# Two attention blocks on one core: K transposed partly in full 128-row tiles, one semaphore and one wait for K and V

## The chip, the core and the metric

The kernel runs on one core of a Trainium2 chip. A core has five engines with instruction streams of their own: TensorE (matmuls, "PE"), VectorE ("DVE"), ScalarE ("ACT"), GpSimd ("POOL") and SyncE ("SP", which here only issues DMAs). They meet through semaphores. Sixteen DMA engines move data between the device's memory (HBM) and the on-chip buffers: SBUF, from which the engines read, and PSUM (8 banks), into which TensorE writes. The metric is the time of one execution on the device in microseconds. Three timed executions of the kernel before took 883.15, 885.32 and 893.99 us; the median, 885.32 us, is its time.

## The reference

Two blocks A and B of the same shapes compute cross attention over a cache; their outputs stand side by side.

```python
B, Sq, D = 16, 64, 640
H, Sk, Dh = 32, 512, 128
def _A_ref(x, k_cache, v_cache, wq, wo):          # B likewise
    q = (x @ wq).reshape(B, Sq, H, Dh).transpose(0, 2, 1, 3)
    scores = jnp.einsum("bhqd,bhkd->bhqk", q, k_cache) * (Dh ** -0.5)
    p = _softmax(scores, axis=-1)
    o = jnp.einsum("bhqk,bhkd->bhqd", p, v_cache)
    return o.transpose(0, 2, 1, 3).reshape(B, Sq, H * Dh) @ wo
return jnp.concatenate([a, b], axis=-1)
```

All is bf16. K and V of the two blocks are 4 x 67.1 MB, most of the 289.41 MB that the kernel reads.

## The kernel before, in words

**Tiling.** A *step* is one head of two batch elements (j = 0 and 1), which share the 128 rows of a tile as two halves of 64 queries. A *macro step* m is two heads (sub = 0 and 1) of the same two batch elements; there are 256. Two macro steps make a *period*, of which there are 128. Eight macro steps (16 heads) make a group, eight groups (all 16 batch elements) a pass, and two passes (the two halves of the heads) a block.

**The operations** of a macro step, by the names that the plan gives them:
- LDK, LDV (SP, L679 and L681): load K and V of the macro step, 512 KB each, in two DMAs (one per j) of 256 KB into rings of 9 and 10 slots. Every half has a semaphore of its own, so the reader waits for two.
- KX (PE, L467): K comes with the keys on the partitions, two heads as rows 0 to 63 and 64 to 127. Each 64x128 piece is transposed by a matmul against the identity; the two heads use the two row halves of the array at the same time. 32 transposes a macro step, head 0 into PSUM bank 6, head 1 into bank 7.
- KE (DVE, L474): copies both banks into the ring `ktp_ring` (2 slots). There is one pair of banks, so the next KX waits for KE.
- SM(m, sub) (PE, L525): the scores of one head, two matmuls of 512 columns, one per j, side by side in the two column halves of the array; one PSUM bank of four for each head.
- MX (DVE, L534), EX (ACT, L540), RC2 (DVE, L546), NM (POOL, L554): maximum, exponential with its sum, reciprocal, and the product with it.
- TR2 (PE, L563): transposes the probabilities in eight full 128x128 tiles. TE2 (DVE, L570, odd macro steps) or TA2 (ACT, L575, even ones) copies them out.
- PV2 (PE, L585): probabilities times V, 16 matmuls of 64 columns; OE4 (ACT, L592) copies a period's result out.
- OP2 (PE, L600): the first 512 columns of the output projection, two matmuls. OX (PE, L610) makes the last 128 columns once a group, 16 matmuls. OVP, OXP (ACT) and OVF, OXF (DVE, L628, L633) copy or add them, and ST (ACT queue, L639) stores them.
- QJ (PE, L482) and QEJ make the queries of the first pass in its first 16 periods; QN (L497) and QEN make those of each next pass, in periods 0 to 111.

**The order** on each engine is written out by hand as tables in `Cfg`: `PE_T`, `ACT_T`, `DVE_T`, `POOL_T`, one row per operation of a period, with its macro step as an offset from the period's first, its sub, and a time in a period of 6.3 us. Only the order within a table sets an engine's program; the times are also used to say which operation reads or writes a buffer first. On PE a period is: SM(0,0), SM(0,1), SM(1,0), QJ, SM(1,1), KX of macro step +2, QN, OP2 -4, TR2 -2, OP2 -3, TR2 -1, KX +3, PV2 -2, OX -3, PV2 -1.

**Loads** are put in order by `build_plan` from due times (`LEAD`, 9 macro steps ahead, or when the ring's slot is free) and paced: every load gets a reckoned time (`DMA_US`), and waits until PE has come to the operation of that time.

**Waits.** `prune_waits` (L331 to L379) drops the waits that another one implies. `run_program` (L689) hangs the last of an operation's waits on its first instruction and issues the others as semaphore instructions ahead of it:

```python
if waits and not op.dma:
    attach = waits.pop()
for s, v in waits:
    e.wait_ge(sems[s], v * (16 if s[0].startswith("d_") else 1))
first, last = emitters[op.kind](e, op)
```

Of the kernel before, what the change touches and what calls it, by code (L numbers as in the profile page):

```python
# [15 lines left out]
class Cfg:  # L16
# [10 lines left out]
    STEP_US = (3.7, 3.2)  # L27
    DMA_US = dict(LDK=0.69, LDV=0.73, LDWQ=1.8, LDWO=1.8, LDX=1.3)
    START_US = -16.0
# [8 lines left out]
    PERIOD = 6.3  # L38
    PE_T = (("SM", 0, 0, 0.0), ("SM", 0, 1, 0.21), ("SM", 1, 0, 0.43), ("QJ", 2, 0, 0.57), ("SM", 1, 1, 0.64),
             ("KX", 2, 0, 2.11), ("QN", -2, 0, 2.12), ("OP2", -4, 0, 2.62), ("TR2", -2, 0, 2.9), ("OP2", -3, 0, 3.06),  # L40
             ("TR2", -1, 0, 3.73), ("KX", 3, 0, 4.07), ("PV2", -2, 0, 4.78), ("OX", -3, 0, 5.02),
             ("PV2", -1, 0, 6.12))
    ACT_T = (("OE4", -4, 0, 0.27), ("ST", -5, 0, 0.58), ("EX", 0, 0, 0.77), ("QEJ", 2, 0, 1.92), ("EX", 0, 1, 2.07),
             ("QEN", -2, 0, 2.33), ("TA2", -2, 0, 4.55), ("EX", 1, 0, 4.56), ("OVP", -3, 0, 5.53), ("EX", 1, 1, 5.92),
             ("OXP", -3, 0, 5.98))
    DVE_T = (("RC2", -1, 0, 0.19), ("MX", 0, 0, 0.5), ("MX", 0, 1, 0.92), ("MX", 1, 0, 1.02), ("KE", 2, 0, 2.2),
             ("MX", 1, 1, 2.54), ("RC2", 0, 0, 3.44), ("TE2", -1, 0, 4.69), ("KE", 3, 0, 5.24), ("OVF", -3, 0, 6.13),
             ("OXF", -3, 0, 6.19))
    POOL_T = (("NM", -1, 0, 0.42), ("NM", -1, 1, 1.5), ("NM", 0, 1, 5.63), ("NM", 0, 0, 5.65))
    ACT_TE = (0,)  # L50
    TRB = (0, 1)
    OXB = 2


class Op:
    __slots__ = ("eng", "kind", "idx", "reads", "writes", "sem", "count", "deps", "waits", "dur", "ts", "aux",
                 "dma")

    def __init__(self, eng, kind, idx, reads=(), writes=(), dur=0.0, ts=None, aux=None):
        self.eng = eng  # L60
        self.kind = kind
        self.idx = idx
        self.reads = tuple(reads)
        self.writes = tuple(writes)
        self.sem = None
        self.count = None
        self.deps = []
        self.waits = []
        self.dur = dur
        self.ts = ts  # L70
        self.aux = aux
        self.dma = kind in ("LDK", "LDV", "LDX", "LDWQ", "LDWO", "ST")


def build_plan(dims, cfg):
# [61 lines left out]
    def make_op(kind, m, sub, ts):  # L137
# [4 lines left out]
        if kind == "KX":  # L142
            return mk("pe", "KX", m, [("kn", m % cfg.NKB, 0), ("kn", m % cfg.NKB, 1), ("ident",)], [("KTB",)], ts)
        if kind == "KE":
# [36 lines left out]
        if kind == "PV2":  # L181
            return mk("pe", "PV2", m, [("pT", m % cfg.NT), ("v", m % cfg.NVB, 0), ("v", m % cfg.NVB, 1)], [("QOB",)],
                      ts)
        if kind == "OE4":
# [69 lines left out]
    for m in range(NMAC):  # L254
        for kind, ring, n_ring, cons, tb in (("LDK", "kn", cfg.NKB, "KX", 1), ("LDV", "v", cfg.NVB, "PV2", 2)):
            ready = at[cons, m - n_ring, 0] if m >= n_ring else NEG
            for j in range(2):
                add(ready, at[cons, m, 0], cfg.LEAD, tb + 0.1 * j, kind, (m, j), [(ring, m % n_ring, j)], (m, j))

# [17 lines left out]
    def sem_key(op):  # L277
        if op.kind in ("LDK", "LDV"):
            return ("d_" + op.kind[2:].lower(), op.writes[0][1], op.aux[1])
        if op.kind == "LDX":  # L280
            return ("d_x", op.aux[1])
        if op.kind in ("LDWQ", "LDWO"):
            return ("d_" + op.kind[2:].lower(), op.writes[0][1])
        if op.kind == "ST":
            return ("d_out",)
        if op.kind in ("INIT1", "INIT2"):
            return ("s_init",)
        return ("s_" + op.kind.lower(),)
# [7 lines left out]
    for eng in ENGINES:  # L296
        for op in progs[eng]:
            if not op.dma:
                assign(op)
    for op in sorted((o for e in ENGINES for o in progs[e] if o.dma), key=lambda o: (o.ts, o.aux)):  # L300
        assign(op)
# [29 lines left out]
def prune_waits(progs):  # L331
# [7 lines left out]
    while done < total:  # L339
        progress = False  # L340
        for eng in ENGINES:
            prog = progs[eng]
            while pc[eng] < len(prog):
# [10 lines left out]
                for w in list(cand):  # L354
                    for o in keep:
                        if o != w and snap[o].get(w[0], 0) >= w[1]:
                            keep.remove(w)
                            break
                op.waits = keep
                for w in keep:  # L360
# [21 lines left out]
def mha_kernel(nc, blocks, out, cfg=None):  # L382
# [32 lines left out]
    with contextlib.ExitStack() as es:  # L415
        block = es.enter_context(nc.Block())

        def sb(name, shape, dt):
            return es.enter_context(nc.sbuf_tensor(name, shape, dt))
# [4 lines left out]
        xT_sb = sb("xT_sb", [128, KT, NBP * 128], BF16)  # L424
        kn_ring = sb("kn_ring", [128, NKB, 2, 8, DH], BF16)
        v_ring = sb("v_ring", [128, NVB, 2, 2, 4, DH], BF16)
        ktp_ring = sb("ktp_ring", [128, NKT, 2, 2, SK], BF16)
        qj_ring = sb("qj_ring", [128, NQ, G, 128], BF16)
# [19 lines left out]
        qo_ps = ps[:, QO_BANK, :]  # L448
        kt_ps = [ps[:, KT_BANK0 + hs, :].bitcast(BF16).rearrange("p (j s) -> p j s", j=2) for hs in range(2)]
        kt_all = ps[:, KT_BANK0:KT_BANK0 + 2, :].rearrange("p b s -> p (b s)").bitcast(BF16)  # L450

# [5 lines left out]

        ox_ps = s_bank(cfg.OXB)[:, 0:N1]

        def em_KX(e, op):  # L460
            m = op.idx
            first = last = None
            for j in range(2):
                for t8 in range(8):
                    for hs in range(2):
                        r = slice(64 * hs, 64 * hs + 64)
                        ins = e.transpose(kt_ps[hs][:, j, 64 * t8:64 * t8 + 64], kn_ring[r, m % NKB, j, t8, :],  # L467
                                          ident[r, 64 * hs:64 * hs + 64])
                        first = first or ins
                        last = ins  # L470
            return first, last

        def em_KE(e, op):
            ins = e.tensor_copy(ktp_ring[:, op.idx % NKT].rearrange("p hs j s -> p (hs j s)"), kt_all)  # L474
            return ins, ins
# [39 lines left out]
        def em_SM(e, op):  # L515
            m, sub = op.idx
            g = 2 * m + sub
            k = g // G
            if k < PPQ:
                q = qj_ring[:, k % NQ, g % G, :]  # L520
            else:
                q = qc_ring[:, qcell[k // PPQ, g % SPB, k % PPQ // (SPB // G)], :]
            first = last = None
            for j in range(2):
                ins = e.matmul(s_bank(g)[64 * j:64 * j + 64, :], q[:, 64 * j:64 * j + 64],  # L525
                               ktp_ring[:, m % NKT, sub, j, :], start=True, stop=True, tile_position=(0, 64 * j))
                first = first or ins
                last = ins
            return first, last
# [48 lines left out]
        def em_PV2(e, op):  # L578
            m = op.idx
            first = last = None  # L580
            for sub in range(2):
                for j in range(2):
                    for t in range(4):
                        col = (2 * (m % 2) + sub) * 128 + 64 * j
                        ins = e.matmul(qo_ps[:, col:col + 64], v_ring[:, m % NVB, j, sub, t, :],  # L585
                                       pT_ring[:, m % NT, sub, t, 64 * j:64 * j + 64], start=(t == 0), stop=(t == 3))
                        first = first or ins
                        last = ins
            return first, last
# [83 lines left out]
        def em_LDKV(e, op):  # L673
            m, j = op.aux
            blk, bp, grp, ps_, hh0 = step_info(2 * m)
            h0 = (ps_ % NHALF) * HH + hh0
            src = blocks[blk][2 if op.kind == "LDV" else 1][2 * bp + j, h0:h0 + 2]
            if op.kind == "LDV":
                ins = e.dma_start(v_ring[:, m % NVB, j], src.rearrange("g (p t) d -> p g t d", p=128))  # L679
            else:  # L680
                ins = e.dma_start(kn_ring[:, m % NKB, j], src.rearrange("hs (p t) d -> (hs p) t d", t=8))  # L681
            return ins, ins
# [3 lines left out]
                        OVP=em_OVP, OXP=em_OXP, OVF=em_OVF, OXF=em_OXF, ST=em_ST, INIT1=em_INIT1, INIT2=em_INIT2,  # L686
                        LDWQ=em_LDWQ, LDWO=em_LDWO, LDX=em_LDX, LDK=em_LDKV, LDV=em_LDKV)

        def run_program(e, prog, final_waits=()):  # L689
            for op in prog:  # L690
# [4 lines left out]
                for s, v in waits:  # L695
                    e.wait_ge(sems[s], v * (16 if s[0].startswith("d_") else 1))
                first, last = emitters[op.kind](e, op)
                if attach is not None:
                    s, v = attach
                    first.wait_op(sems[s], v * (16 if s[0].startswith("d_") else 1), "sem-ge")  # L700
                last.then_inc(sems[op.sem], 16 if op.dma else 1)
# [73 lines left out]
```

## Time and profile before

| what | value | where from |
|---|---|---|
| median of the timed executions | 885.32 us | the three times |
| profiled execution | 887.1 us, span 885.3 us | its own time; the span is from its first to its last instruction |
| mean granted TensorE clock | 0.996 | of full speed |
| PE, DVE, ACT, POOL busy | 94%, 82%, 74%, 47% of the span | the page, part 1 |
| KX, one matmul; one weight load | 191 ns; 95 ns, 8192 of each | groups at L467 |
| KE | 1215 ns, 256 of them | group at L474 |
| a 256 KB load of K or V | 5.7 us from issue to landing | DMA issues |
| HBM read | 289.41 MB; 336 GB/s moved in the mean | DMA parts |

A matmul's mean is its time from start to modelled end; matmuls overlap, so the rate is read from the distance between starts. "Busy" of a group is the union of its instructions' times. "Idle before" is the time its engine stood before them, with what ended it; "issue" there means that nothing in the profile explains it. The chain goes back from the last instruction to what released each one.

### The profile page before, as it was taken

The page shows a single profiled execution, that of the slowest core. Times are in us where ns is not written, and L with a number is a line of the kernel's source. Part 1 is how long each engine was busy: PE and PEld are TensorE (multiplying, and loading weights), DVE is VectorE, ACT ScalarE, POOL GpSimd, SP SyncE. Part 2 cuts the span into 40 slices and gives each one's busy share as a digit, 9 for nine tenths or more (in the row PEclk, how much of TensorE's full clock was granted, in tenths as well). Part 3 has the DMA queues.
Part 4 walks back from the last instruction along what each step waited for, and adds up shares of the span by engine and source line. Part 5 has one row for each costly group of instructions (what it writes and reads, how often), then busy time and mean ns, then how long its engine had stood idle before and what let it go on. Part 6 is the DMA issues. An engine that isn't in the chain of part 4 may idle for free.

```text
span 885.3 us, 40110 instructions
## 1 busy us (share of the span) xinstructions
PE 835.7 (94%) x17264; PEld 575.4 (65%) x17264; DVE 729.9 (82%) x1184; ACT 657.4 (74%) x1497; POOL 418.6 (47%) x518
## 2 busy tenths in 40 slices
PE   4989998999989999999999999999999999999897
PEld 3666775666656666665666666676666666766665
DVE  3667777888878888888888888888889889889996
ACT  2667777877877777777776787787788867877775
POOL 1333434544544454454444455455454544555454
PEclk8999999999999999999999999999999999999999
DMA  9999999999999999999999999999999999999980
GB/s 256 336 318 305 345 361 357 347 363 361 367 358 341 368 346 284 360 362 365 344 305 348 358 364 355 365 357 363 350 352 341 366 367 335 328 334 370 351 262 17
DMA packets 244847, 297.28 MB, mean 336 GB/s; under 512 B 27584, under 2 KB 179136, under 8 KB 244672
## 3 DMA queue, kind: packets, MB, share of 16 engines
q1 hardware_dynamic: 242368, 292.10, 98.9%
q8 instruction: 138, 2.26, 1.0%
q10 hardware_dynamic: 2304, 2.62, 0.8%
q14 instruction: 37, 0.30, 0.1%
HBM read 289.41 MB, written 2.62 MB: 330 GB/s over the span
## 4 chain that ended last, share of the span: by engine, by line
PE 87%; DMA 4%; DVE 4%; issue 3%; SPq 1%; ACT 0%; ACTq 0%
PE ps L467 16%; PE ps L585 14%; PE ps L497 14%; PE ps L525 14%; PE ps L563 12%; PE ps L600 12%; PE ps L610 3%; PE ps L482 2%; DVE ktp_ring L474 2%; DVE negmax L534 2%; DMA wq_sb<-in_A_wq_dram 1%; DMA kn_ring<-in_A_k_cache_dram 1%; DMA v_ring<-in_A_v_cache_dram 1%; SPq L679 0%; DVE pT_ring L570 0%
## 5 line engine op out<-in xcount | busy, mean ns | idle before, releaser
L554 POOL TENSOR_SCALAR pn_ring<-p_ring,recip 128x512 bf16<-128x512 bf16 x512 | 418.0, 846 | 458.7 <-DVE recip L546 358.2
L540 ACT ACTIVATE p_ring<-ps,negmax 128x512 bf16<-128x512 f32 x512 | 347.3, 684 | 75.6 <-DVE negmax L534 67.3
L534 DVE TENSOR_REDUCE negmax<-ps 128x1 f32<-128x512 f32 x512 | 328.2, 683 | 32.0 <-PE ps L525 27.4
L474 DVE COPY ktp_ring<-ps 128x2048 bf16<-128x2048 bf16 x256 | 311.1, 1215 | 32.6 <-PE ps L467 32.2
L467 PEld LDWEIGHTS ps<-ident,kn_ring 64*128 64x128 bf16 x8192 | 135.5, 95 | 80.5 <-issue 64.8
L467 PE MATMUL ps<-ident,kn_ring 64*128 64x64 bf16 x8192 | 167.5, 191 | 15.6 <-issue 9.2
L563 PEld LDWEIGHTS ps<-ident,pn_ring 128*128 128x128 bf16 x2048 | 135.3, 98 | 63.9 <-ACT p_ring L540 3.7
L585 PE MATMUL ps<-pT_ring,v_ring 128*128 128x64 bf16 x4096 | 151.7, 193 | 9.7 <-issue 8.2
L575 ACT ACTIVATE pT_ring<-ps 128x1024 bf16<-128x1024 bf16 x128 | 131.1, 1024 | 39.3 <-PE ps L563 38.8
L563 PE MATMUL ps<-ident,pn_ring 128*128 128x128 bf16 x2048 | 156.5, 219 | 2.5 <-issue 2.2
L570 DVE COPY pT_ring<-ps 128x1024 bf16<-128x1024 bf16 x128 | 88.3, 690 | 81.9 <-PE ps L563 81.9
L600 PE MATMUL ps<-wo_sb,oT_ring 128*128 128x512 bf16 x512 | 152.5, 379 | 3.2 <-issue 1.8
L497 PE MATMUL ps<-xT_sb,wq_sb 128*128 128x512 bf16 x560 | 141.0, 381 | 4.1 <-issue 4.1
L585 PEld LDWEIGHTS ps<-pT_ring,v_ring 128*128 128x128 bf16 x4096 | 131.6, 98 | 19.5 <-issue 11.1
L525 PE MATMUL ps<-ktp_ring,qc_ring 128*64 128x512 bf16 x896 | 122.5, 387 | 2.6 <-issue 2.4
L592 ACT ACTIVATE oT_ring<-ps 128x512 bf16<-128x512 f32 x128 | 76.4, 597 | 48.9 <-PE ps L585 40.0
L540 ACT ACTIVATION_READ_ACCUMULATOR p_ring<-ps,negmax 128x1 f32 x512 | 103.1, 201 | 0.0
L510 ACT ACTIVATE qc_ring<-ps 128x256 bf16<-128x256 f32 (+1 forms) x168 | 70.3, 453 | 43.7 <-PE ps L497 43.7
L497 PEld LDWEIGHTS ps<-xT_sb,wq_sb 128*128 128x128 bf16 x560 | 45.5, 98 | 50.5 <-issue 5.8
L600 PEld LDWEIGHTS ps<-wo_sb,oT_ring 128*128 128x128 bf16 x512 | 43.2, 98 | 31.6 <-issue 2.8
L525 PEld LDWEIGHTS ps<-ktp_ring,qc_ring 128*64 128x64 bf16 x896 | 37.3, 108 | 40.3 <-issue 25.8
L546 DVE RECIPROCAL recip<-rowsum 128x2 f32<-128x2 f32 x256 | 39.6, 154 | 3.7 <-ACT p_ring L540 3.7
(18 smaller groups left out, 175.4 us busy)
## 6 DMA issues: line engine op xcount, KB each, us to landing
kn_ring<-in_A_k_cache_dram SPq DMA_DIRECT2D x256, 256.0 KB, 5.7
v_ring<-in_A_v_cache_dram SPq DMA_DIRECT2D x256, 256.0 KB, 5.7
kn_ring<-in_B_k_cache_dram SPq DMA_DIRECT2D x256, 256.0 KB, 5.8
v_ring<-in_B_v_cache_dram SPq DMA_DIRECT2D x256, 256.0 KB, 5.7
wq_sb<-in_A_wq_dram SPq DMA_DIRECT2D x8, 640.0 KB, 7.0
wo_sb<-in_A_wo_dram SPq DMA_DIRECT2D x8, 640.0 KB, 6.5
wq_sb<-in_B_wq_dram SPq DMA_DIRECT2D x8, 640.0 KB, 7.1
wo_sb<-in_B_wo_dram SPq DMA_DIRECT2D x8, 640.0 KB, 7.6
```

The costliest lines, as they stand in the source:

```text
L467: ins = e.transpose(kt_ps[hs][:, j, 64 * t8:64 * t8 + 64], kn_ring[r, m % NKB, j, t8, :], ident[r, 64 * hs:64 * hs + 64])
L474: ins = e.tensor_copy(ktp_ring[:, op.idx % NKT].rearrange("p hs j s -> p (hs j s)"), kt_all)
L497: ins = e.matmul(qo_ps, wq_sb[:, qslot(hh // G), kt, (hh % G) * DH:(hh % G + 1) * DH], xT_sb[:, kt, b0 * 128:(b0 + QB) * 128], start=(kt = ...
L525: ins = e.matmul(s_bank(g)[64 * j:64 * j + 64, :], q[:, 64 * j:64 * j + 64], ktp_ring[:, m % NKT, sub, j, :], start=True, stop=True, tile_ ...
L534: ins = e.reduce_max(negmax[:, r:r + 1], s_bank(g), axis=AX.X, negate=True)
L540: ins = e.activation(p_ring[:, g % NP, :], s_bank(g), ACTF.Exp, bias=negmax[:, r:r + 1], scale=1.0, accum_out=rowsum[:, r:r + 1])
L554: ins = e.tensor_scalar(dst, src, recip[:, r:r + 1], 1.0, ALU.mult, ALU.mult)
L563: ins = e.transpose(pt_flat(m)[:, (4 * sub + t) * 128:(4 * sub + t + 1) * 128], pn_ring[:, g % NPN, t * 128:(t + 1) * 128], ident[:, :])
L570: ins = e.tensor_copy(pT_ring[:, m % NT].rearrange("p s t q -> p (s t q)"), pt_flat(m))
L575: ins = e.activation(pT_ring[:, m % NT].rearrange("p s t q -> p (s t q)"), pt_flat(m), ACTF.Copy)
L585: ins = e.matmul(qo_ps[:, col:col + 64], v_ring[:, m % NVB, j, sub, t, :], pT_ring[:, m % NT, sub, t, 64 * j:64 * j + 64], start=(t == 0), ...
L600: ins = e.matmul(out_ps, oT_ring[:, m // 2 % NO, 2 * (m % 2) + sub, :], wo_sb[:, wslot(ps_, hh // G), hh % G, 0:N0], start=(hh == 0), stop ...
```

## The change

- **K of every fourth macro step in full tiles.** `KFULL = (3,)`: where m % 4 is 3, KX makes 16 transposes of 128x128 (both heads at once) in place of 32 of 64x128. Bank 6 then holds j = 0 and bank 7 j = 1, with the two heads in turns of 64 columns, so SM reads its 512 columns in eight pieces of 64. KE copies the same 2048 columns in the same order. It is always the KX at offset +3 of every other period.
- **One semaphore and one wait for K and V.** K of a macro step is one DMA of 512 KB; V stays two DMAs of 256 KB, issued one behind the other, which count on one semaphore (32 in place of 16). `DMA_US` doubles for both; pacing is per macro step.
- **Waits put ahead.** Where an operation on PE keeps more than one wait, one that doesn't depend on the operation before it is hung on the last instruction of that operation (`early`). With that, PE has two semaphore instructions left, where the trace of before has 771.
- **The tables.** PE's order is the same. ACT: QEJ stands ahead of EX(0,0) and EX(0,1) rather than between them, and ST moves from offset -5 behind OE4 to -9 behind EX(1,1). DVE: MX(1,1) stands ahead of KE +2 and MX(1,0) behind it (before: the other way round), and OVF moves from the period's end to behind MX(1,0). POOL: NM of macro step -1 goes sub 1, sub 0.

PE's program falls from 17,264 matmuls to 16,240, each with a weight load.

```diff
-    DMA_US = dict(LDK=0.69, LDV=0.73, LDWQ=1.8, LDWO=1.8, LDX=1.3)
+    DMA_US = dict(LDK=1.38, LDV=1.46, LDWQ=1.8, LDWO=1.8, LDX=1.3)
-    ACT_T = (("OE4", -4, 0, 0.27), ("ST", -5, 0, 0.58), ("EX", 0, 0, 0.77), ("QEJ", 2, 0, 1.92), ("EX", 0, 1, 2.07),
+    ACT_T = (("OE4", -4, 0, 0.04), ("QEJ", 2, 0, 0.75), ("EX", 0, 0, 2.59), ("EX", 0, 1, 2.63), ("QEN", -2, 0, 2.66),
+             ("TA2", -2, 0, 3.43), ("EX", 1, 0, 4.6), ("OVP", -3, 0, 4.64), ("EX", 1, 1, 5.63), ("ST", -9, 0, 5.67),
-    DVE_T = (("RC2", -1, 0, 0.19), ("MX", 0, 0, 0.5), ("MX", 0, 1, 0.92), ("MX", 1, 0, 1.02), ("KE", 2, 0, 2.2),
+    DVE_T = (("RC2", -1, 0, 0.65), ("MX", 0, 0, 1.77), ("MX", 0, 1, 1.93), ("MX", 1, 1, 2.55), ("KE", 2, 0, 2.91),
+             ("MX", 1, 0, 3.05), ("OVF", -3, 0, 4.41), ("RC2", 0, 0, 4.58), ("TE2", -1, 0, 5.0), ("KE", 3, 0, 5.48),
...
+    KFULL = (3,)
...
-            return mk("pe", "KX", m, [("kn", m % cfg.NKB, 0), ("kn", m % cfg.NKB, 1), ("ident",)], [("KTB",)], ts)
+            return mk("pe", "KX", m, [("kn", m % cfg.NKB), ("ident",)], [("KTB",)], ts)
...
-                op.waits = keep
+                if (eng == "pe" and len(keep) > 1 and pc[eng] and prog[pc[eng] - 1].early is None):
+                    before = prog[pc[eng] - 1]
+                    for w in keep:
+                        if snap[w].get(before.sem, 0) < before.count:
+                            before.early = w
+                            break
+                op.waits = [w for w in keep if pc[eng] == 0 or eng != "pe" or w != prog[pc[eng] - 1].early]
...
+                    kt = kn_ring[:, m % NKB, j, t8 * DH:(t8 + 1) * DH]
+                    if k_full(m):
+                        last = e.transpose(kt_full[j][:, 128 * t8:128 * t8 + 128], kt, ident[:, :])
+                        first = first or last
+                        continue
...
+            if k_full(m):
+                kt = ktp_ring[:, m % NKT].rearrange("p (j t hs s) -> p j t hs s", j=2, t=8, hs=2)
+                kt = [kt[:, j, :, sub] for j in range(2)]
...
+                return tuple(e.dma_start(v_ring[:, m % NVB, j], vs[j]) for j in range(2))
+            ins = e.dma_start(kn_ring[:, m % NKB], src.rearrange("j hs (p t) d -> (hs p) j (t d)", t=8))
...
+                if op.early is not None:
+                    assert last is not first
+                    last.wait_op(sems[op.early[0]], full(*op.early), "sem-ge")
```

## The prediction

> **What bounds the kernel now.** I read the page from its top: the shares of the engines, the DMA queues, the chain that ended last, then the groups.
>
> ```profile
> span 885.3 us, 40110 instructions
> PE 835.7 (94%) x17264; PEld 575.4 (65%) x17264; DVE 729.9 (82%) x1184; ACT 657.4 (74%) x1497; POOL 418.6 (47%) x518
> ...
> q8 instruction: 138, 2.26, 1.0%
> ...
> PE 87%; DMA 4%; DVE 4%; issue 3%; SPq 1%; ACT 0%; ACTq 0%
> ...
> L467 PE MATMUL ps<-ident,kn_ring 64*128 64x64 bf16 x8192 | 167.5, 191 | 15.6 <-issue 9.2
> L563 PE MATMUL ps<-ident,pn_ring 128*128 128x128 bf16 x2048 | 156.5, 219 | 2.5 <-issue 2.2
> ```
>
> PE carries 87% of the chain, at a granted clock of 0.996. The DMA engines are busy throughout, but they aren't the bound: comparing landings with first uses in the trace, K and V lie ready 11 to 21 us before use from 110 us on. Only in the first 80 us does PE wait for data.
>
> PE runs nearly gap-free, so the question is where it still loses time. The view of waits, PE alone:
>
> ```profile
> PE ps L467 <- issue: 9.2, 14, 1.2
> PE ps L585 <- issue: 8.2, 17, 1.3
> ...
> PE ps L497 <- issue: 4.1, 4, 1.7
> PE ps L467 <- DMA kn_ring<-in_A_k_cache_dram: 3.3, 3, 1.9
> PE ps L467 <- DVE ktp_ring L474: 2.6, 2, 1.3
> ```
>
> The largest entry is "issue": PE stands though nothing it waits for is late. The timeline shows one, in the middle of a PV2 of 16 matmuls:
>
> ```profile
> 401.22 0.64 PE L467 MATMUL ps<-ident,kn_ring 64*128 64x64 bf16 x32
> ...
> 401.79 0.61 PE L585 MATMUL ps<-pT_ring,v_ring 128*128 128x64 bf16 x15
> ...
> 403.04 0.75 PE L585 MATMUL ps<-pT_ring,v_ring 128*128 128x64 bf16 x17 [0.64 <-issue]
> ```
>
> Counting PE's records (weight loads, matmuls, semaphore waits), the stands at 402.2, 415.1 and 429.2 us come after records 15,552, 16,064 and 16,576, and all the other long ones also at multiples of 256 from there. Queue q8 moved 138 packets of 16,384 B, which is 256 instructions of 64 B: PE stands for its own next block of code. For the 128 block ends after 60 us I took from the trace X, from the passing of one block end to the start of the next q8 packet (mean 3.07 us, 10th to 90th percentile 1.5 to 4.3); 2.45 us from that start until PE goes on, where it stood; and T, PE's own time for the 256 instructions (mean 5.90). A stand of X + 2.45 - T, where positive, sums to 39.5 us; the gaps themselves sum to 41.6. So about 40 us of the span are waits for code, and they depend on how many instructions PE runs per microsecond.
>
> **The change, part by part.**
>
> *Fewer PE instructions.* 64 of the 256 KX shrink from 32 transposes to 16, each a weight load and a matmul: 64 x 32 = 2,048 records less. The 771 semaphore instructions of PE fall to about 2, as one of two waits moves to the last instruction of the step before and K and V have one wait each. 35,301 records become 32,484, 137.9 blocks become 126.9. With the PE costs below (21.6 us) T becomes (5.90 x 137.9 + 21.6) / 126.9 = 6.58, 0.68 more. Taking 0.68 from each of the 128 stands leaves some 10.5 us of 39.5, times 127/138 is 10. X may rise: a K or V half is now issued some 0.7 us sooner, which puts about 0.12 MB more in flight on 2.2 MB, and over the block ends X rises 1.26 us per MB: 0.15. With T ahead by 0.53 instead, 13.6 are left. I take 13.5: **-26 us**; -30 with X as it is, +2 with X 0.8 later (a rival).
>
> *Full tiles.* All 64 are the KX at offset 3 of every other period, between a TR2 and a PV2. From single matmul starts: TR2's last to KX's first 152 ns, 450 within KX, KX's last to PV2's first 122: 724. The full form is not in the trace; its nearest row is TR2 itself (128x128, same identity): 55.8 ns from start to start, and TR2 to OP2, both full-width, 56. So 56 + 15 x 55.8 + 56 = 949, **+225 ns**. The switch of tile shape, about 95 ns on each side, is thus credited. 64 x 0.225 = 14.4; in the last 16 periods, without QN, PE has slack (DVE is in the chain there), which takes 8: **+12.6**. If the shape switches were still paid, +24.
>
> The scores of such a step read K in 64-column pieces 128 apart. Nothing in the trace streams like that. Bounds: nothing, or half speed, 64 x 2 x 0.213 = 27 us; nearest row, PV2's 64-column matmuls at 29.1 ns, eight of them 233 ns against 216, gives 2. I take 0, as the row is still a stream of whole columns.
>
> *The waits put ahead.* SM(0,1)'s second matmul now waits for KE (DVE); behind it stand SM(1,0) and all of PE. This is where PE and DVE are level:
>
> ```profile
> 354.11 0.69 DVE L570 COPY pT_ring<-ps 128x1024 bf16<-128x1024 bf16 x1 [0.50 <-PE ps L563]
> ...
> 354.72 1.21 DVE L474 COPY ktp_ring<-ps 128x2048 bf16<-128x2048 bf16 x1
> ...
> 355.62 1.08 PE L525 MATMUL ps<-ktp_ring,qc_ring 128*64 128x512 bf16 x8
> ...
> 356.05 0.17 PEld L525 LDWEIGHTS ps<-ktp_ring,qc_ring 128*64 128x64 bf16 x4 [0.29 <-issue]
> ```
>
> TE2 waits for TR2, KE follows it and ends at 355.93; SM(1,0) loads its weights at 356.05. Today that delays the matmul by only 8 ns (0.463 us after SM(0,0) instead of 0.456), and 62 of 103 periods show it. SM(0,1)'s second half would start at 0.243, KE ends at 0.317: with 0.08 for the release it starts at 0.40, and its half of the array, 0.213 per step, ends SM(1,1) 0.12 later than now. Behind a full KX, KE starts 0.286 later (KX's last start + 0.257, the delay that TE2 has behind TR2) while PE is only 0.225 later: 0.18. Some 39 x 0.18 + 23 x 0.12 = 10; stands for code in between cover a part: **+9**, bounds 0 and 13.
>
> The other early waits: KX's last waits for TA2 (in the traced period done 0.18 us before), and KE stands behind it; PV2's last waits for TE2 (done 0.2 before), OP2's for NM (done 1.6 before), TR2's for K (landed 11 us before). They hold nothing that PE didn't hold. PV2 to PV2 loses 3.9 us today in late TE2; behind a later KX about half: **-2**.
>
> *K in 512 KB.* The queue has 4,096 small semaphore packets less (9.5 ns each, 16 engines: 2.4 us each, all hidden behind the 11 us lead). SP issues 256 DMAs fewer and was itself waiting for PE some 320 us. In the first 80 us, where there is no lead, the order of bytes is nearly the same; bounds -3 and +3, I take 0.
>
> *Orders on ACT, DVE, POOL.* QEJ before EX matters in the first 16 periods alone; QN needs QEJ only after SM(1,1) and KX (1 us). MX(1,1) and MX(1,0) swap around KE, and EX(1,0) stands behind TA2, which ends later. The store goes out three periods later; OVF of the next group waits for it to land (5.1 us) and has about that; OVF now ahead of TE2 adds up to 0.7 us of DVE, 16 times, in periods with OX, where PE works 0.9 us longer. Cost 0; up to +5 if that cover fails.
>
> Sum against the profiled span: 885.3 - 26 + 12.6 + 9 - 2 = 878.9. The profiled execution took 887.1, 1.8 around its span; the median of the runs is 885.32, the span's own number, so I forecast **879 us**.
>
> **The rivals.**
>
> *Code comes later (slower).* In the 10 ns before a q8 packet there start 0.89 semaphore packets (4 B) of the data queue, against 0.20 by chance: the code waits until a data DMA's share on its engine is through. A share is 16 KB now, 32 KB for K after. Where a weight load (640 KB, 40 KB a share) was in flight X was 3.48 instead of 2.92. If the code waits behind a fixed number of shares (X is about four of 0.7 us), every third grows double: 3.07 x 4/3, +0.8 to +1.0, and the stands stay at 41: 885.3 + 12.6 + 9 + 2 = 909. It decides from X + 0.6 on. Against it: X follows bytes in flight, which hardly change. 13%. (The Trainium skill, "DMA: Bandwidth & Descriptors", Queues, rings and completion order, says an engine alternates between queues a packet at a time, which agrees with the semaphore packet just ahead, but would make X less than one share; the trace has four.)
>
> *Early waits free, stands nearly gone.* KE is released in time and X stays: 885.3 - 30 + 12.6 - 2 = 866, or 860 with a better start. 17%.
>
> *The stands aren't for code, or don't depend on its amount.* If PE's code buffer ran many blocks ahead, fewer instructions would win nothing: 885.3 + 12.6 + 9 = 907. For it, that most block ends pass without a stand; against it, the multiples of 256 and the sum above. 4%. (The Trainium skill, "Runtime: NRT & Kernel Launch", Instruction fetch mechanics, gives PE 128 KiB, 2,048 instructions, refilled in 16 KiB blocks and mostly hidden; the blocks agree, the hiding doesn't.)
>
> *K in pieces at half speed*: 879 + 27 = 906. 3%. Something else, either sign: 3%. My forecast, 866 to 893: 60%.
>
> **Numbers.** 2% is about what a measurement of this kernel can tell from no change: 867.6 and 903.0. Faster, most of the second rival and half of the rest: 0.16. Slower, most of the other three: 0.15. Same: 0.69. The range leaves out a tenth on each side: 862 to 899; the forecast's own is 866 to 893.
>
> **What would show it.** q8 packets 127; PE's "issue" waits of 27.9 us down to about 10; KX full 16 matmuls 55.8 ns apart, with no 122 ns behind it; SM(0,1)'s two halves about 0.16 apart, then SM(1,1) late by 0.12 to 0.18; KE to SM unchanged in OX periods. X well over 3.3, or SM matmuls of a full K longer than 387 ns, would make me wrong on the slow side; both halves of SM(0,1) together and stands under 5 us on the fast side.

## The result and the profile after

The changed kernel takes **880.84 us**, the median of 20 executions (879.90 to 882.98), against 885.37 us for the kernel before (20 executions, 879.70 to 895.75): a ratio of 0.9956, 95% interval 0.9940 to 0.9972. By the 2% that the forecast named this is "no change", and the forecast of 879 us is 0.2% off. The ratios here are of the fast runs alone (of the 20 executions of before, four that lie over 1.5% above its quickest are left out), so they differ by up to 0.3% from the quotients of the medians. The span fell by 7.0 us; the sum had said 6.4. As the trace shows, though, two of its terms were wrong by 14 and 8 us in opposite directions, and smaller misses made up what that left.

The page of the kernel after, from top to bottom the parts shown of before (engines, code queue, chain, groups; the last two columns of a group are busy time with the mean of one, and the idle time ahead with what ended it):

```profile
span 878.3 us, 36911 instructions
...
PE 856.7 (98%) x16240; PEld 603.1 (69%) x16240; DVE 733.4 (84%) x1184; ACT 657.0 (75%) x1497; POOL 419.1 (48%) x518
...
q8 instruction: 127, 2.08, 1.0%
...
PE 86%; DVE 9%; DMA 4%; ACT 1%; issue 0%; SPq 0%; ACTq 0%
...
L484 PE MATMUL ps<-ident,kn_ring 64*128 64x64 bf16 x6144 | 123.9, 191 | 1.5 <-DVE ktp_ring L489 1.3
...
L479 PE MATMUL ps<-ident,kn_ring 128*128 128x128 bf16 x1024 | 67.7, 219 | 1.3 <-DVE ktp_ring L489 1.3
```

PE's busy share rose to 98%, although it runs 1,024 matmuls less; "issue", 3% of the chain before, is 0%; the code queue moved 127 packets, as forecast. KX (L467 before) is now two groups: L484 in pairs, L479 in full tiles. Its idle time ahead, 15.6 us before, is 1.5 and 1.3.

PE's waits after, in the view that headed the prediction (us in total, times, longest):

```profile
PE ps L497 <- DMA wq_sb<-in_A_wq_dram: 7.2, 1, 7.2
PE ps L606 <- DMA v_ring<-in_A_v_cache_dram: 2.3, 2, 1.5
...
PE ps L546 <- DVE ktp_ring L489: 1.5, 2, 0.8
```

No "issue" is left in it; 27.9 us stood there before. What remains in it is mostly the start, where PE waits for data. VectorE's share of the chain went from 4% to 9%: from 780 us on, when QN is done, MX, KE and TE2 hold 63% of the chain, against 27% before. Nothing in the list looks like a new cost. The new cost shows in the timeline of a steady period (L546 is SM, L489 KE, L591 TE2):

```profile
351.97 0.69 DVE L591 COPY pT_ring<-ps 128x1024 bf16<-128x1024 bf16 x1 [0.70 <-PE ps L584]
...
352.58 1.22 DVE L489 COPY ktp_ring<-ps 128x2048 bf16<-128x2048 bf16 x1
...
353.48 0.14 PEld L546 LDWEIGHTS ps<-ktp_ring,qc_ring 128*64 128x64 bf16 x3
353.48 1.21 PE L546 MATMUL ps<-ktp_ring,qc_ring 128*64 128x512 bf16 x8
...
353.85 0.35 PEld L546 LDWEIGHTS ps<-ktp_ring,qc_ring 128*64 128x64 bf16 x5 [0.23 <-DVE ktp_ring L489]
```

Before, SM's eight matmuls took 1.08 us, and four weight loads went ahead of the wait for KE. Now three do: the fourth weight load, that of SM(0,1)'s second half, stands at 353.85 until KE (ended 353.80) is through, and SM takes 1.21 us. As PE is "busy" with the other half meanwhile, the loss is counted as busy time and not as a wait.

To account for the whole span I added up, from the starts of PE's matmuls, each operation's time from its first start to the next operation's first start, over periods 9 to 126, with the stands at code block ends taken out and put in a row of their own (us):

| | before | after | difference | the sum's term |
|---|---|---|---|---|
| stands at block ends | 40.6 | 0.9 | -39.7 | -26 |
| KX and TR2 | 251.9 | 265.8 | +13.9 | +12.6 |
| SM | 118.9 | 135.9 | +17.0 | +9 |
| PV2 | 123.9 | 123.1 | -0.8 | -2 |
| QN | 111.5 | 113.1 | +1.6 | 0 |
| OP2, OX, QJ | 135.9 | 136.2 | +0.3 | 0 |
| outside these periods | 102.5 | 103.2 | +0.7 | 0 |

Together -7.0. (Counted over the whole run after 60 us, the stands before are 41.0; the prediction had 41.6.) Code and full tiles alone would have given -26; the wait that was put ahead took most of that back.

### The profile page after: what moved, and what is told of

Its sections match the earlier page's. It is cut to its first block, busy times and chain, and to the rows that moved or that the text cites. A ratio compares the mean times of both kernels' runs of the same rounds, so it can differ in the third digit from the quotient of the medians.

```text
span 878.3 us, 36911 instructions
## 1 busy us (share of the span) xinstructions
PE 856.7 (98%) x16240; PEld 603.1 (69%) x16240; DVE 733.4 (84%) x1184; ACT 657.0 (75%) x1497; POOL 419.1 (48%) x518
## 4 chain that ended last, share of the span: by engine, by line
PE 86%; DVE 9%; DMA 4%; ACT 1%; issue 0%; SPq 0%; ACTq 0%
PE ps L546 15%; PE ps L512 15%; PE ps L606 13%; PE ps L584 11%; PE ps L484 11%; PE ps L621 11%; PE ps L479 6%; DVE negmax L555 4%; DVE ktp_ring L489 4%; PE ps L631 3%; PE ps L497 2%; DMA v_ring<-in_A_v_cache_dram 2%; DVE pT_ring L591 1%; DMA kn_ring<-in_A_k_cache_dram 1%; DMA out_dram<-out_sb 1%; DMA wq_sb<-in_A_wq_dram 1%
## 5 line engine op out<-in xcount | busy, mean ns | idle before, releaser
L489 DVE COPY ktp_ring<-ps 128x2048 bf16<-128x2048 bf16 x256 | 311.6, 1217 | 23.5 <-PE ps L479 11.8
L596 ACT ACTIVATE pT_ring<-ps 128x1024 bf16<-128x1024 bf16 x128 | 131.1, 1024 | 31.5 <-PE ps L584 31.3
L606 PE MATMUL ps<-pT_ring,v_ring 128*128 128x64 bf16 x4096 | 147.1, 193 | 3.0 <-DMA v_ring<-in_A_v_cache_dram 2.3
L591 DVE COPY pT_ring<-ps 128x1024 bf16<-128x1024 bf16 x128 | 88.0, 688 | 73.5 <-PE ps L584 73.5
L484 PEld LDWEIGHTS ps<-ident,kn_ring 64*128 64x128 bf16 x6144 | 101.1, 95 | 58.1 <-issue 49.7
L606 PEld LDWEIGHTS ps<-pT_ring,v_ring 128*128 128x128 bf16 x4096 | 132.4, 98 | 7.0 <-DMA v_ring<-in_A_v_cache_dram 2.5
L546 PE MATMUL ps<-ktp_ring,qc_ring 128*64 128x512 bf16 x896 | 136.1, 389 | 0.1
L484 PE MATMUL ps<-ident,kn_ring 64*128 64x64 bf16 x6144 | 123.9, 191 | 1.5 <-DVE ktp_ring L489 1.3
L546 PEld LDWEIGHTS ps<-ktp_ring,qc_ring 128*64 128x64 bf16 x896 | 44.2, 108 | 43.7 <-DVE ktp_ring L489 24.7
L479 PE MATMUL ps<-ident,kn_ring 128*128 128x128 bf16 x1024 | 67.7, 219 | 1.3 <-DVE ktp_ring L489 1.3
```

Of the source, the lines that this page charges most:

```text
L479: last = e.transpose(kt_full[j][:, 128 * t8:128 * t8 + 128], kt, ident[:, :])
L484: last = e.transpose(kt_ps[hs][:, j, 64 * t8:64 * t8 + 64], kt[r], ident[r, 64 * hs:64 * hs + 64])
L489: ins = e.tensor_copy(ktp_ring[:, op.idx % NKT], kt_all)
L596: ins = e.activation(pT_ring[:, m % NT].rearrange("p s t q -> p (s t q)"), pt_flat(m), ACTF.Copy)
```

## The experiments

The theory after this reading: (1) the full tiles cost PE time but win more by less code; (2) the early waits, with the single wait for K, win by taking 767 semaphore instructions out of PE's code (the version without early waits, below, has 127 of them gone), but one of them, for KE, costs 10 to 17 us; (3) the size of K's load and the store's new place cost nothing. The rivals: the early waits alone free PE, or it is the waits and not the amount of code. The ratios below are all to the kernel before on the same chip (medians there 888.27 us for the first four, 889.52 for the next four, 890.62 for the last; three chips). The changed kernel itself has no runs beside these on record; the nearest to it is the version with K in halves, on the first of these chips. A difference of a few us between medians from different chips says little by itself.

### KE's wait left where it was

Of an operation's waits that may go ahead, take another one than KE's, if there is one. For SM(1,0) that is the wait for EX (96 times) or for OXP (16 times); KE's stays on SM(1,0), and no other operation's waits change.

```diff
-                    for w in keep:
+                    for w in sorted(keep, key=lambda w: w[0] == ("s_ke",)):
```

> The changed kernel, but where SM(1,0) keeps two waits it is the one for EX that goes ahead to SM(0,1)'s second matmul; the wait for KE stays on SM(1,0)'s own first matmul. No semaphore instruction comes back (2 as before), no matmul moves. Theory (the wait for KE put ahead costs 20 us of skewed score matmuls where the kernel before lost 6): both halves of SM(0,1) start 3 ns apart again, and the time falls by 14 us, to about 867. Rival (the skew is harmless, since PE would wait at that place anyway): 879 to 882.

Measured: **870.84 us**, ratio 0.9817 (0.9766 to 0.9868). SM in the timeline and as a group, first this kernel:

```profile
350.58 1.22 DVE L489 COPY ktp_ring<-ps 128x2048 bf16<-128x2048 bf16 x1
...
351.48 1.05 PE L546 MATMUL ps<-ktp_ring,qc_ring 128*64 128x512 bf16 x8
...
351.85 0.20 PEld L546 LDWEIGHTS ps<-ktp_ring,qc_ring 128*64 128x64 bf16 x4 [0.23 <-DVE ktp_ring L489]
```
```profile
L546 PE MATMUL ps<-ktp_ring,qc_ring 128*64 128x512 bf16 x896 | 120.5, 388 | 0.3
```

and the same group in the changed kernel:

```profile
L546 PE MATMUL ps<-ktp_ring,qc_ring 128*64 128x512 bf16 x896 | 136.1, 389 | 0.1
```

KE runs at the same place to 0.01 us (0.90 ahead of SM's first start in both) and the same weight load waits for it. Only now four loads go ahead and four wait, as before the change; SM's busy time falls by 15.6 us with the mean matmul unchanged. In the account SM is 119.8 us, 16.1 less than in the changed kernel. So the KE wait, and its place alone, cost SM 16 us. The medians fell by 10.0 (by 10.9 from the version with K in halves, on the same chip) and the span by 7.9, not by 16: in the account stands are +1.4, QN, PV2, OP2 and OX +2.9, KX and TR2 +0.4, and 3.6 us more lie outside the steady periods (period 9 begins at 91.6 instead of 88.0 us). This version beats both kernels.

### No full tiles

```diff
-    KFULL = (3,)
+    KFULL = ()
```

> The changed kernel with all K transposed as 64-row pairs (KFULL empty): 2,048 PE records more, 134.9 blocks of code instead of 126.9, PE's own time for a block about 6.15 us instead of 6.69. Theory A (code now comes early because the semaphore instructions are gone, X about 2.1 us): still nearly no stands for code, so the 12.6 us of the full tiles and 4 us of the later KE are won: about 864. Theory B (the stands went because PE asks for fewer instructions per microsecond, with X about 3.1): some 26 us of stands come back, 885 to 892.

Measured: 873.99 us, ratio 0.9854 (0.9803 to 0.9904), between the two theories' times. The account, against the changed kernel: KX and TR2 -13.9 (back to 251.9), SM -5.2 (no KE is late by a full KX), stands +10.5 (T 6.14, 12.0 us in all after the first 60 us), PV2 +2.1. In the kernel as changed, the full tiles thus cost 7 us rather than win: the early waits have taken most of the stands away already.

### No early waits

```diff
-                if (eng == "pe" and len(keep) > 1 and pc[eng] and prog[pc[eng] - 1].early is None):
+                if (False and eng == "pe" and len(keep) > 1 and pc[eng] and prog[pc[eng] - 1].early is None):
```

> The changed kernel without waits put ahead: 642 semaphore instructions on PE again, 129.4 blocks of code; full tiles, K in 512 KB and tables stay. The skew of the score matmuls goes (-14 us). Theory A (semaphore instructions hold PE's sequencer back, so that the next block is asked for late): X returns from 2.1 to about 3.1 us and some 14 us of stands for code come back, about 881. Theory B (only the amount of code counts): nearly no stands, about 867.

Measured: 886.10 us, ratio 0.9983 (0.9952 to 1.0014). PE has 644 semaphore instructions again (771 before; the single wait for K saves the rest); the stands are 15.3 us, SM 124.6 (5.7 over before: a KE behind a full KX now reaches SM(1,0) late by itself). The waits list has its "issue" entries again:

```profile
PE ps L606 <- issue: 3.6, 5, 1.6
...
PE ps L484 <- issue: 1.6, 5, 0.5
```

So the early waits are worth 4 to 5 us as they were made (881.71 with K in halves, on the same chip, and 880.84), and 15 us (886.10 to 870.84, same chip) with KE's left out.

### K in two loads of 256 KB again

With one semaphore and one wait still; only the loads are halved.

```diff
-            ins = e.dma_start(kn_ring[:, m % NKB], src.rearrange("j hs (p t) d -> (hs p) j (t d)", t=8))
-            return ins, ins
+            ks = src.rearrange("j hs (p t) d -> (hs p) j (t d)", t=8)
+            return tuple(e.dma_start(kn_ring[:, m % NKB, j], ks[:, j]) for j in range(2))
```

> The changed kernel with K of a macro step loaded in two DMAs of 256 KB on the one semaphore, as V is. Everything else stays. Theory (the size of the K loads has no part in the gain): 880 to 882 and X as in the changed kernel, 2.1 us. Rival (larger shares on each DMA engine change when code comes): X moves by 0.5 us or more, to either side; with X up, up to 10 us of stands, 890. In the first 80 us, where PE waits for data, at most 3 us either way.

Measured: 881.71 us, ratio 0.9939 (0.9909 to 0.9969), the span 878.4 against 878.3; X 2.16 against 2.12 us, stands 2.0 against 1.9. The size of the load plays no part, neither in the stands nor elsewhere.

### The store back in its old place

The version with KE's wait left, with ST at -5 behind OE4 again.

```diff
-    ACT_T = (("OE4", -4, 0, 0.04), ("QEJ", 2, 0, 0.75), ("EX", 0, 0, 2.59), ("EX", 0, 1, 2.63), ("QEN", -2, 0, 2.66),
-             ("TA2", -2, 0, 3.43), ("EX", 1, 0, 4.6), ("OVP", -3, 0, 4.64), ("EX", 1, 1, 5.63), ("ST", -9, 0, 5.67),
+    ACT_T = (("OE4", -4, 0, 0.04), ("ST", -5, 0, 0.58), ("QEJ", 2, 0, 0.75), ("EX", 0, 0, 2.59), ("EX", 0, 1, 2.63), ("QEN", -2, 0, 2.66),
+             ("TA2", -2, 0, 3.43), ("EX", 1, 0, 4.6), ("OVP", -3, 0, 4.64), ("EX", 1, 1, 5.63),
```

> The kernel of e1_ke_late with the store put back where the kernel before has it (offset -5, behind OE4). In e1_ke_late OVF stood 4.6 us in all for stores that had not landed, 7 times, and SM 2.6 us for OXF. Theory (the late store costs time once PE is faster): these 4.6 us of DVE go, and 2 to 5 us of the time: 866 to 869 beside 871. Rival (OVF stands where PE has time to spare): no difference, 870 to 872.

With KE late, DVE's waits showed this line (OVF, L649, waits until the store has landed), which in the changed kernel is 1.3 us in 2 waits:

```profile
DVE out_sb L649 <- DMA out_dram<-out_sb: 4.6, 7, 1.1
```

Here it is gone, and the time is 871.08 us, ratio 0.9788 (0.9761 to 0.9814), against 870.84 (0.9817 on another chip, the intervals overlap): no gain that these runs can tell. The stands at block ends are 7.7 us here and 3.3 there, so that a gain of up to 4 us could be hidden behind them; more than that OVF's wait did not cost.

### Full tiles alone

The kernel before, with KX, KE's layout and SM as in the changed kernel for m % 4 = 3, and nothing else of the change.

```diff
+    KFULL = (3,)
...
+                    if k_full(m):
+                        last = e.transpose(kt_full[j][:, 128 * t8:128 * t8 + 128], kn_ring[:, m % NKB, j, t8, :],
+                                           ident[:, :])
+                        first = first or last
+                        continue
```

> The kernel before with the full tiles alone (KFULL = (3,)); its 771 semaphore instructions, its loads and tables stay. 129.9 blocks of code instead of 137.9; PE's own time for a block about 6.42 us instead of 5.91. Theory (fewer instructions pay for longer streaming): stands for code fall from 41 to about 15 us, the tiles cost 13 and the later KE 4: 876 to 880 beside 885 to 888 for the kernel before on this chip. Rival (full tiles cost and the code doesn't depend on them): 13 to 18 us slower than the kernel before, about 902.

Measured: 877.62 us, ratio 0.9852 (0.9822 to 0.9883), with all 771 semaphore instructions still there.

```profile
q8 instruction: 130, 2.13, 1.0%
...
PE 89%; DMA 4%; issue 3%; DVE 3%; SPq 1%; ACT 0%; ACTq 0%
```

The 3% of "issue" are mostly not stands: this trace lacks 129 matmul records, nearly all of QN, and each shows as a gap. (So do the traces of the store back, of no full tiles with KE's wait left, and of the first padding.) Counted at the block ends, with the records put back by their weight loads, the stands are 14.5 us against 41.0, with T 6.42: -26.5. By T times the blocks, PE does the same work in 19 us *more* (834 against 815; some 14 of it in KX and TR2, 5 in SM behind a later KE), and the kernel is faster: fewer instructions are the gain, the rest of the change isn't needed for it. The ratio to the kernel before is even better than that of the whole change (0.9852 against 0.9956, the intervals apart).

One comparison doesn't fit. The version without early waits has the same full tiles and, beyond this kernel, only the larger load of K, the one wait for K and V, and the new tables. Its T (6.47) and its stands (15.3 us) are close to this kernel's, and yet it took 886.10 us (ratio 0.9983), 8.5 us more. Of the 8.0 us between the two spans, 2.7 lie before period 9, 3.2 in periods 16 to 61 and 2.0 in the periods from 112 on. No run has those parts of the change alone, so their cost without the early waits isn't shown.

### KE's wait left and no full tiles

```diff
-    KFULL = (3,)
+    KFULL = ()
...
-                    for w in keep:
+                    for w in sorted(keep, key=lambda w: w[0] == ("s_ke",)):
```

> The kernel of e1_ke_late with all K as 64-row pairs: 134.9 blocks of code, PE's own time for a block about 6.08 us. Theory (full tiles buy with 13 us of streaming about as much of stands for code): stands of 12 to 15 us come back, 868 to 873, no difference that 2% tells from e1_ke_late. Rival (code comes in time anyway once the early waits are there): stands stay under 4 us and the tiles' 13 us are won, about 858.

Measured: 871.27 us, ratio 0.9783 (0.9758 to 0.9807), the same as with full tiles (870.84), with 135 blocks and 19.3 us of stands against 127 and 3.3: 16 more, against 14 us of PE time saved. With the early waits done well, full tiles are an even exchange.

### Padding, first try: in the narrow streams

The version with KE's wait left, plus semaphore instructions on PE whose value has long been reached: one in the middle of each half of KX and TR2, eight in each PV2. They should bring the code back to 139 blocks at no cost of their own.

```diff
+        def pad(e):
+            e.wait_ge(sems[("s_init",)], 1)
+            e.wait_ge(sems[("d_x", 0)], 16)
...
+                        if t % 2:
+                            pad(e)
```

> The kernel of e1_ke_late with 12 semaphore instructions a macro step more on PE, each a wait that was fulfilled long before, spread over KX, TR2 and PV2: 138.9 blocks of code instead of 126.9, PE's own time for a block about 6.02 us instead of 6.59; no work, order or real wait changes. Theory (the amount of code counts): 10 to 30 us of stands come back at block ends, 881 to 900. Rival (only waits that hold the sequencer count): no stands, 870 to 873.

Measured: 968.44 us, ratio 1.0871 (1.0840 to 1.0903), far outside what either theory allowed. The stands are 23.9 us; the rest is PV2 itself. Its line in the timeline, a pair of PV2, and its group:

```profile
380.99 2.03 PE L616 MATMUL ps<-pT_ring,v_ring 128*128 128x64 bf16 x32
```
```profile
L616 PE MATMUL ps<-pT_ring,v_ring 128*128 128x64 bf16 x4096 | 235.3, 191 | 2.6 <-DMA v_ring<-in_A_v_cache_dram 0.2 <-DVE pT_ring L599 0.2
```

In the changed kernel the same 32 matmuls take 1.11 us, and the group is busy for 147.1 us. As its padding was not free, the test can't settle what the amount of code costs, though the stands did rise by 20.6 us with 12 blocks more.

### Padding, second try: between wide matmuls

Now only between QN's five matmuls and OP2's two, twice `pad` in each gap.

```diff
+        def pad(e):
+            for _ in range(2):
+                e.wait_ge(sems[("s_init",)], 1)
+                e.wait_ge(sems[("d_x", 0)], 16)
...
+                if kt < KT - 1:
+                    pad(e)
```

> The kernel with KE's early wait left out (870.8 us, stands 3.3 us, T 6.59, X 2.90), with 2,816 more semaphore instructions on PE, each on a semaphore that has long had its value: four between each two of QN's five matmuls and four between OP2's two. A matmul of 512 columns takes 216 ns there, and four such instructions at the 33 ns that the padded PV2 shows take 133, so they should cost nothing themselves. PE's records come back to 35,302, the number of the kernel before (137.9 blocks). Theory, the stands depend on how much code PE runs: T falls to about 6.1, the stands come back to 10 to 15 us as where the full tiles are left out (12.0 at T 6.14), and the time is 878 to 884; q8 moves 138 packets. Rival, the amount of code is nothing and the early waits win by taking semaphore instructions out of the narrow streams: 869 to 873 with 138 packets. If the instructions aren't hidden behind the wide matmuls: 2,816 x 33 ns, some 930 or more.

Each two waits came out as one instruction (of the 67 ns below, not 33), so there are 1,408 and not 2,816 of them: 132.4 blocks and not 137.9. Measured: 879.50 us, ratio 0.9901 (0.9874 to 0.9927).

```profile
q8 instruction: 132, 2.16, 1.0%
```
```profile
PE ps L489 <- issue: 6.9, 10, 1.2
```

The padded operations themselves are unchanged (QN's median 1,090 ns, OP2's 432 in both). SM is 118.7 us, as good as without padding. The stands went from 3.3 to 16.5 us, and the median up by 8.7 (7.5 by the two ratios, whose intervals lie apart; the chips differ): instructions that do nothing and wait for nothing, and stand where they are free, cost some 8 us by being code. L489, KX in pairs, is where most of it shows: 64 instructions in 573 ns, the quickest use of code in the kernel.

All the kernels side by side (block ends after the first 60 us; X from one block end to the start of the next code packet, T PE's own time for 256 instructions; times are medians from four sets of runs, in which the kernel before took 885.4, 888.3, 889.5 and 890.6 us):

| kernel | PE blocks | T, us | X, us | stands, us | time, us |
|---|---|---|---|---|---|
| before | 137.9 | 5.91 | 3.07 | 41.0 | 885.4 |
| full tiles alone | 129.9 | 6.42 | 2.77 | 14.5 | 877.6 |
| changed | 126.9 | 6.69 | 2.12 | 1.9 | 880.8 |
| changed, K in halves | 126.9 | 6.69 | 2.16 | 2.0 | 881.7 |
| changed, no full tiles | 134.9 | 6.14 | 2.92 | 12.0 | 874.0 |
| changed, no early waits | 129.4 | 6.47 | 2.96 | 15.3 | 886.1 |
| KE's wait left | 126.9 | 6.59 | 2.90 | 3.3 | 870.8 |
| and the store back | 126.9 | 6.56 | 2.98 | 7.7 | 871.1 |
| and no full tiles | 134.9 | 6.08 | 3.07 | 19.3 | 871.3 |
| and padding, wide | 132.4 | 6.26 | 3.10 | 16.5 | 879.5 |
| and padding, narrow | 138.9 | 6.58 | 3.17 | 23.9 | 968.4 |

The q8 packets of all eleven are these block counts, rounded.

## Why the prediction was right, point by point

**Stands for code, -26: right in kind, mis-sized; -39.7.** That they are code and depend on its amount is shown by the full tiles alone (2,048 instructions less, 26.5 us of stands less) and by the wide padding (1,408 more, 13.2 more). T was foreseen well (6.58; measured 6.69). X was not: I let it rise by 0.15 to 3.22, and it fell to 2.12. Even where it stayed near 3 (2.90 with KE's wait left) 3.3 us were left and not 10.5, because its spread shrank too: 10th to 90th percentile 1.82 to 3.72, and 1.47 to 4.33 before. I had moved the old distribution as it was.

**Full tiles, +12.6: right; +13.9.** TR2's last to KX's first 56 ns, 15 steps of 55.8, KX's last to PV2's first 56: 949 ns against 724, as worked out. Of the 2 us that I took off for slack in the last periods nothing shows. SM's reading of K in pieces is not at half speed: of the four SM matmuls on such a K the first takes 403 ns, the others 379, as all do on the K of pairs; 64 x 24 ns would be 1.5 us. The shape switches are gone, as credited: 96 ns ahead of KX (152 against 56) and some 93 behind it (122 against PV2's own step of 29). That agrees with the Trainium skill, "TensorEngine Tiling (Array Packing)", Key Properties, by which changing the mode drains TensorE; the price is from the trace, as no figure stands there.

**KE's wait, +9 (bounds 0 and 13): the mechanism right, the size wrong; +17.0.** SM(0,1)'s halves start 0.13 us apart behind a pair (foreseen 0.16) and 0.21 behind a full KX, and SM takes 0.20 us longer behind a full KX, 0.12 behind a pair (0.18 and 0.12). What failed was the count: I took the 62 of 103 periods in which KE was late before, 39 of them behind full tiles. It is late in all periods but those behind an OX, 77 of the same 103, 52 of them behind full tiles, and in the last 16 periods, which I had left out. 52 x 0.20 + 25 x 0.12 is 13.4 for these 103 alone. Moving this one wait back took SM from 135.9 to 119.8.

**The other early waits, 0:** right to about 1 us. The list of waits after shows 0.7 us for TE2 and 0.6 for TA2. **PV2 to PV2, -2:** -0.8.

**K in 512 KB, 0:** right; the halved loads give the same span to 0.1 us. (The lead of the loads, from a tile's last landing to its first use, is 8 to 22 us for K and 7 to 25 for V in the trace of before, and not 11 to 21; the term doesn't hang on it.) **Orders, 0:** right in sum (QN +1.6, outside the periods +0.7), and putting the store back won nothing that shows. Both hold beside the early waits; without them, the comparison under "Full tiles alone" leaves 8.5 us open.

**The rivals.** *Code comes later* fell with X at 2.12, and the halved K loads show that the size of a load doesn't set X. *The stands don't depend on the amount of code* fell with the padding. *K in pieces at half speed* fell. *Early waits free, stands nearly gone*, 866 us, came true by half: the stands did go. It needed KE's wait to be free; with that wait left alone the kernel takes 870.8.

So the number was right in part by luck: two terms missed by 14 and 8 us in opposite directions, which left 6 us, and the small terms missed by 5 us the other way (KX and TR2 1.3, PV2 1.2, QN 1.6, the rest 1.0). That code stands would shrink with PE's instructions, that full tiles would cost PE time and that KE's wait would hold half of the array was all borne out. The bounds of the KE term were not sound, as they came from one traced period and from how often that had happened before.

**What stays open:** why X is 2.1 us in the changed kernel and with K in halves, and 2.8 to 3.2 in all others. It is not the load's size. Fewer bytes are in flight in the changed kernel than with KE's wait left (2.0 and 2.7 MB in the mean between 110 and 780 us, from issue to landing), but before also had 2.0, with X above 3. Within a run X rises with them by 0.4 to 0.9 us per MB in this count, with much scatter. Also open is why some versions begin period 9 at 88 us and others at up to 91.6, and what the one wait for K and V and the tables cost where no wait is put ahead.

## What to carry to other kernels

Where an engine runs narrow instructions, count them: 256 instructions that take less time than the fetch of the next 256 cost a stand, and an operation that is slower but has half the instructions can win. (It won here in the kernel before, and was an even exchange once other instructions were gone: do the sum anew after each such step.) A wait moved ahead to save an instruction must be one whose event is long past; hang the early one, never the one that comes last, and take the choice from when each releaser ends, not from its place in a list. A half of an array that stands while the other half works is booked as busy: look at starts and at group times, not only at waits.

## What the runs showed of the hardware

- **A fulfilled semaphore instruction costs PE's sequencer time.** In the narrowly padded PV2 the matmuls start 29 ns apart for about the first ten, and from then on in turns of 28 and 97: 125 ns for two matmuls and one semaphore instruction (of two waits) in place of 58, 67 ns each. My reading is that PE works off a lead first, and that then the sequencer sets the pace. Between matmuls of 512 columns, 216 ns apart, two such instructions cost nothing (QN takes 1,090 ns with and without them).
- **Code isn't free on TensorE.** A stand of X + 2.45 - T where that is positive gave 39.5 of 41.0 us before. The Trainium skill, "Runtime: NRT & Kernel Launch", Instruction fetch mechanics, holds the fetch hidden because the sequencer issues more slowly than the blocks come. The traces of this case differ and show the margin: T 5.9 to 6.7 us for a block against X + 2.45 of 4.6 to 5.6, with stands of up to 41 us of the span where the two come near.
- **Two column halves of the array drift apart.** In the changed kernel SM(0,1)'s second half starts 0.13 us behind its first, and its half of the array stays behind until SM's end (starts at 0, 0, 0.24, 0.37, 0.46, 0.61, 0.67, 0.83 us). The first half doesn't wait for it, nothing shows as idle, and KX behind SM begins only when both are through, 0.31 us after the last of these starts, as with KE's wait left, where the last start is at 0.68 to 0.70.
